# A convolution's stationary tile with its row pitch changed from 512 to 536 values, beside attention

## The chip, the cores and the metric

The kernel runs on one core of a Trainium2 chip. The metric is the device time of one execution in microseconds (us). Work is spread over five engines that run side by side: TensorE (PE, matmuls, with its weight loads listed as PEld), VectorE (DVE), ScalarE (ACT), GpSimd (POOL) and SyncE (SP, which here only issues DMAs). SBUF is the on-chip memory of 128 partitions from which the engines read, PSUM the one into which PE writes.

## The reference

Two independent blocks, whose outputs stand side by side in 1024 columns. All inputs are bf16, the sequence has S = 2048 rows and D = 512 columns.

Block A is attention with 32 heads of 16 values:

```
qkv = x @ wqkv                       # 2048x512 @ 512x1536
p = softmax(q k^T * 16**-0.5)        # per head, 2048x2048
a = concat_heads(p @ v) @ wo         # 2048x512
```

Block B is a short convolution with 4 taps, a gate, a long causal convolution and another gate, per column d:

```
k_shift[t] = sum of 4 taps of k around t, with weights shift_k[d]
kv = k_shift * v
y[t] = sum over s <= t of kv[s] * ssm_k[d, t - s]  +  kv[t] * ssm_D[d]
b = q * y
```

The reference computes the long convolution with Fourier transforms; the kernel computes it with matmuls.

## The kernel before

**Attention.** The scores are made in blocks of 128 keys x 512 queries for one head: 2048 blocks, taken in 692 chunks of three (in the first 56 chunks, of three and two by turns). For each chunk T, `emit_qk` (line 494) issues the QK matmuls into three PSUM banks; one ACT instruction (line 501) takes the exponential of the chunk into PT; two steps later `emit_pv` (line 566) multiplies by V. Chunks alternate between two sets of three banks, so the QK matmuls of chunk T wait until ACT is done with chunk T - 2. In many groups of 64 blocks, four blocks are taken from ACT and their exponential is computed on DVE by a polynomial (lines 519 to 535, with the tiles EI, EM, EH and PTD); in those chunks ACT has 1024 values per partition in place of 1536.

**Long convolution.** For each of the 512 columns d the kernel multiplies a Toeplitz matrix by the column of kv. The product kv lies in KV, `[128, NB, C]`: 128 positions on the partitions, NB = 16 blocks of 128 positions, C = 512 columns. For each d, `load_wr` (line 658) reads 128 shifted copies of the reversed kernel row from scratch memory in DRAM into one of the R_W = 12 rows of the ring WR, 512 KB each. Then come 16 lags n = 0 to 15: the stationary operand is `KV[:, n:NB, d]`, so 16 - n columns, one value from each block; the moving operand is 128 columns of WR. Four neighbouring columns d make a group and lie in four column groups of PE; the 128 groups run in order. `conv_lags` (line 669) issues lags n0 to n1 of a group:

```
ins = e.matmul(PS[32 * c:32 * c + NB - n, BGB, col:col + 128],
               lhsT=KV[:, n:NB, d],
               rhs=WR[:, d % R_W, 128 * (NB - 1 - n):128 * (NB - n)], ...
```

So a load for lag n reads 16 - n values of 2 bytes per partition, each C values further on than the last. When a group is done, its four rows of WR are loaded anew. After eight groups `conv_turn` (line 699) transposes the result, and DVE multiplies it by q and writes it back over the used columns of KV (line 712). `store_y` (line 715) sends it out, in 8 DMAs for each half of the columns.

**Before that,** KV holds the input x: four DMAs (`load_x`, line 191) bring it in, PE transposes it (`turn_x`, line 268, loads at line 276), and later DVE writes kv over it (`kv_chunk`, line 370, the write at line 385).

**Order of the work.** It is written out ahead by a planner in the kernel's own code. A loop over chunks T emits QK, PV and then `emit_bg(T)` (line 794): a unit of the attention's own projections, or up to LAGS = 5 lags of the convolution. The planner has times of its own for the loads of WR and for the chunks; when less than five lags come out, small matmuls on a zero tile ZR (`keep_busy`, line 773, matmul at line 780; their load has 16 columns that lie side by side) fill up. Each engine runs its list in order, with semaphores between them. All tiles are allocated at the start, one behind the other: KV comes after xT, KTo, QT, VAF, PT and WR and ahead of all others.

Of the kernel before, what the change touches and what calls it, by code (L numbers as in the profile page):

```python
# [23 lines left out]
C = 512  # L24
NB = S // 128
PAD = 128
LKZ = PAD + S
R_W = 12
R_PT = 4
R_O = 16  # L30
# [63 lines left out]
def bass_concat_heads__mha_block__ssm_conv_h3__prompt_kernel(  # L94
# [12 lines left out]
    x2, q2, k2, v2, out2 = A_x[0], B_q[0], B_k[0], B_v[0], out[0]  # L107
    kz_ap = nc.dram_tensor("kz_scratch", (C, LKZ), BF16).ap()

    ctxs = []  # L110

    def enter(cm):
        ctxs.append(cm)
        return cm.__enter__()

    def sem(name):
        return enter(nc.semaphore(name))

    def sb(name, shape, dt=BF16):
        return enter(nc.sbuf_tensor(name, shape, dt))  # L120
# [5 lines left out]
    VAF = sb("VAF", [128, KT, VROW])  # L126
    PT = sb("PT", [128, R_PT, 3 * QB])
    WR = sb("WR", [128, R_W, S])
    KV = sb("KV", [128, NB, C])
    QN = sb("QN", [128, NB, CH])  # L130
    WQP = sb("WQP", [128, 4, NG, 128])
    WKV = sb("WKV", [128, 2, 4, D])
# [18 lines left out]
    wr_flat = WR[:, :, :].rearrange("p r w -> p (r w)")  # L151
    KZS = wr_flat[:, 0:4 * LKZ].rearrange("p (c m) -> p c m", c=4)
    DSS = wr_flat[:, 4 * LKZ:4 * LKZ + 4].rearrange("p (c m) -> p c m", m=1)
    o1 = 5 * S
# [10 lines left out]
    pe, act, dve, pool, sp = [Eng(sem(n)) for n in ("s_pe", "s_act", "s_dve", "s_pool", "s_sp")]  # L165

    def dma(eng, dsem, outp, inp, deps=(), transpose=False):
        h = dsem.add()

        def fn(e):  # L170
            f = e.dma_start_transpose if transpose else e.dma_start
            f(outp, inp).then_inc(dsem.sem, 16)  # L172
        eng.op(fn, deps, inc=False)
        return h

    d_w = [DmaSem(sem(f"d_w{i}")) for i in range(5)]
    d_x = [DmaSem(sem(f"d_x{i}")) for i in range(4)]
# [6 lines left out]
    d_outA = [DmaSem(sem(f"d_outA{i}")) for i in range(R_A)]  # L184
    d_wr = [DmaSem(sem(f"d_wr{i}")) for i in range(R_W)]


    wview = A_wqkv.rearrange("(c p) f -> p c f", p=128)
    h_xn = [None] * 4

    def load_x(sc):
        h_xn[sc] = dma(sp, d_x[sc], KV[:, 4 * sc:4 * sc + 4, :],
                       x2[sc * 512:(sc + 1) * 512, :].rearrange("(t p) d -> p t d", p=128))
    load_x(0)
    h_wq = [dma(act, d_w[0], WST[:, :, 0:128], wview[:, :, 0:128])]
    h_wk = [dma(act, d_w[1], WK[:, :, 0:128], wview[:, :, D:D + 128])]
    load_x(1)
    h_wv = dma(act, d_w[2], WV, wview[:, :, 2 * D:3 * D])
    h_shk = dma(act, d_tap, SHK[:, :, :], B_shift_k.rearrange("(c p) m -> p c m", p=128))
# [12 lines left out]
    def load_kv(j, h_edge=None):  # L212
        b = kvbuf[(7 - j) % 3]
        deps = [h_kvfree.get(j + 3), h_edge]
        if j == 0:
            z = wr_flat[0:3, o1 + 5120 + 1024:o1 + 5120 + 4096]
            deps = [pool.op(lambda e: e.memset(z, 0.0), deps)]
        r0 = 2 * j * 128
        dma(sp, d_kv[j], b[4], v2[r0:r0 + 256, :].rearrange("(t p) d -> p t d", p=128), deps)
        for m in range(4):  # L220
            q = sp if m == 3 else pool
            ds = d_kv[j] if m == 3 else d_kp[j]
            if j == 0 and m > 0:
                h = dma(q, ds, b[m][m:128, 0, :], k2[0:128 - m, :], deps)
                src = bass.AP(tensor=k2.tensor, offset=k2[128 - m, 0].offset, ap=[[D, 128], [1, D]])
                h = dma(q, ds, b[m][:, 1, :], src, deps)
            else:
                src = bass.AP(tensor=k2.tensor, offset=k2[r0 - m, 0].offset, ap=[[D, 128], [128 * D, 2], [1, D]])
                h = dma(q, ds, b[m], src, deps)
            if m >= 2:  # L230
                h_kv[(j, m - 2)] = h
# [36 lines left out]
    def turn_x(sc, cp, bank, eng):  # L268
        pbf = PS[:, bank, :].bitcast(BF16)

        def fn(e):
            ins = None
            for i in range(2):
                for t in range(4):
                    c = 2 * cp + i
                    ins = e.transpose(pbf[:, 512 * i + 128 * t:512 * i + 128 * t + 128],
                                      KV[:, 4 * sc + t, 128 * c:128 * c + 128], IDN[:, :])
            return ins
# [11 lines left out]
    def pe_unit(u, bank, dcs=(0, 1, 2, 3)):  # L290
        kind = u[0]
        deps = [bank_free[bank]]
        if kind == "q":
            _, qb, g = u
            deps += h_x[qb] + [h_wqp[g]]

            def mm(e, dc):
                return e.matmul(PS[:, bank, :], lhsT=WQP[:, dc, g, :], rhs=xT[:, dc, qb * 512:(qb + 1) * 512],  # L298
                                start=(dc == 0), stop=(dc == 3))
        elif kind == "k":  # L300
            _, o, sc = u
            deps += h_x[sc] + [h_wk[min(o, 1)]]

            def mm(e, dc):
                return e.matmul(PS[:, bank, :], lhsT=WK[:, dc, o * 128:(o + 1) * 128],  # L305
                                rhs=xT[:, dc, sc * 512:(sc + 1) * 512], start=(dc == 0), stop=(dc == 3))
        else:
            _, kt = u
            deps += h_x[kt // 4] + [h_wv]

            def mm(e, dc):
                return e.matmul(PS[:, bank, :], lhsT=xT[:, dc, kt * 128:(kt + 1) * 128], rhs=WV[:, dc, :],  # L312
                                start=(dc == 0), stop=(dc == 3))

        def fn(e):
            ins = None
            for dc in dcs:
                ins = mm(e, dc)
            return ins
        return pe.op(fn, deps)  # L320
# [49 lines left out]
    def kv_chunk(j):  # L370
        b = kvbuf[(7 - j) % 3]
        st = {}

        def tap(m):
            in1 = TB[:, m:m + 1, :].broadcast_to([128, 2, D])
            st[m] = dve.op(lambda e: e.tensor_tensor(b[m], b[m], in1, ALU.mult),  # L376
                           [h_kv[(j, 0)], h_kv[(j, 1)], h_tb[m]])

        def add(m):
            st["a"] = dve.op(lambda e: e.tensor_tensor(b[3], b[3], b[m], ALU.add), [st[m], st[3], st.get("a")])  # L380

        def last():
            h = None
            for i in range(2):
                h = dve.op(lambda e, i=i: e.tensor_tensor(KV[:, NB - 1 - 2 * j - i, :], b[3][:, i, :], b[4][:, i, :],
                                                          ALU.mult), [st["a"], h_xt[0]])
            h_kvfree[j] = h
            h_kvc[0] = h
            if j >= 3:
                load_kv(j - 3)  # L390
        return [lambda m=m: tap(m) for m in (3, 2)] + [lambda: add(2), lambda: tap(1), lambda: add(1),
                                                       lambda: tap(0), lambda: add(0), last]
# [31 lines left out]
    h = pe_unit(("k", 0, 0), 7)  # L424
# [200 lines left out]
    def op_mm(qb, t, g0, g1, bank):  # L625
        dd = [h_wop[0], bank_free[bank] if g0 == 0 else None]
        dd += [h_otn[(qb * NG + g, 2 * (t // 2) + 2)] if g == NG - 1 and qb == NQB - 1 else h_otn[qb * NG + g]
               for g in range(g0, g1)]

        def fn(e):  # L630
            ins = None
            for g in range(g0, g1):
                ins = e.matmul(PS[:, bank, :], lhsT=OTN[:, oslot(qb * NG + g), t * 128:(t + 1) * 128], rhs=WOP[:, g, :],  # L633
                               start=(g == 0), stop=(g == NG - 1))
            return ins
        return pe.op(fn, dd)
# [21 lines left out]
    def load_wr(d):  # L658
        r = d % R_W
        deps = [h_kzw[0], h_kvc[0]] if d < R_W else [h_wrfree[d - R_W]]  # L660
        src = bass.AP(tensor=kz_ap.tensor, offset=kz_ap[d, 0].offset, ap=[[1, 128], [1, S]])
        h_wr[d] = dma(sp, d_wr[r], WR[:, r, :], src, deps)
# [6 lines left out]
    def conv_lags(qd, n0, n1):  # L669
# [5 lines left out]
        def fn(e):  # L675
            ins = None
            for n in range(n0, n1):
                for c in range(4):
                    d = 4 * qd + c
                    ins = e.matmul(PS[32 * c:32 * c + NB - n, BGB, col:col + 128],  # L680
                                   lhsT=KV[:, n:NB, d],
                                   rhs=WR[:, d % R_W, 128 * (NB - 1 - n):128 * (NB - n)],
                                   start=(n == 0), stop=(n == NB - 1), tile_position=(0, 32 * c))
            return ins
        h = pe.op(fn, deps)
        if n1 == NB:
            for c in range(4):
                h_wrfree[4 * qd + c] = h
                if 4 * qd + c + R_W < C:
                    load_wr(4 * qd + c + R_W)  # L690
# [8 lines left out]
    def conv_turn(b):  # L699
# [9 lines left out]
        yv = bass.AP(tensor=pbf.tensor, offset=pbf[:, NB - 1:NB].offset, ap=[pbf.ap[0], [-1, NB], [32, 32]])  # L709
        dst = KV[:, :, 32 * b:32 * b + 32]  # L710
        qv = QN[:, :, 32 * b % CH:32 * b % CH + 32]
# [3 lines left out]
    def store_y(i, t, hh):  # L715
        dst = out2[:, D + CH * i:D + CH * (i + 1)].rearrange("(t p) c -> p t c", p=128)
        dma(sp, d_outB[i], dst[:, t:t + 2, :], KV[:, t:t + 2, CH * i:CH * i + CH], [hh])

# [175 lines left out]
    for t in range(4):  # L894
        h = op_mm(qb, t, 7, 8, banks[t])
# [55 lines left out]
```

## Time and profile before

| What | Value |
|---|---|
| Runs | 925.15, 921.75, 929.33 us; median 925.15 |
| The profiled execution's own time | 924.61 us |
| Its span from the first to the last instruction | 922.8 us |
| Mean granted clock of TensorE | 0.993 |
| First exponential starts | 11.6 us |
| Convolution's matmuls | 126.9 to 880.5 us |
| Last exponential starts | 911.4 us |
| Data moved by DMA | 295.69 MB, 320 GB/s on the mean |

A row of a group gives source line, engine, operation, tile written and tile read, partitions x values, count; then busy time in us, mean duration of one in ns, idle time of the engine before them and who ended it. A form such as 128*16 on a load or matmul is 128 rows by 16 columns of the stationary operand. Loads and matmuls overlap, and so do successive activations: their durations don't add up to time. How fast ACT goes is read from the distance between starts. A row of the timeline has start in us, duration in us, then the same names and a count of merged instructions.

A row of the waits says who waited for whom, us in total, how often, the longest. A row of the windows has the stretch, its length, the busy time of PE, PEld, DVE, ACT and POOL with counts, granted clock, DMA share and GB/s.

### The profile page before, as it was taken

The page shows a single profiled execution, that of the slowest core. Times are in us where ns is not written, and L with a number is a line of the kernel's source. Part 1 is how long each engine was busy: PE and PEld are TensorE (multiplying, and loading weights), DVE is VectorE, ACT ScalarE, POOL GpSimd, SP SyncE. Part 2 cuts the span into 40 slices and gives each one's busy share as a digit, 9 for nine tenths or more (in the row PEclk, how much of TensorE's full clock was granted, in tenths as well). Part 3 has the DMA queues.
Part 4 walks back from the last instruction along what each step waited for, and adds up shares of the span by engine and source line. Part 5 has one row for each costly group of instructions (what it writes and reads, how often), then busy time and mean ns, then how long its engine had stood idle before and what let it go on. Part 6 is the DMA issues. An engine that isn't in the chain of part 4 may idle for free.

```text
span 922.8 us, 29902 instructions
## 1 busy us (share of the span) xinstructions
PE 758.8 (82%) x13615; PEld 349.7 (38%) x13664; DVE 638.9 (69%) x835; ACT 890.8 (97%) x698; POOL 38.2 (4%) x59
## 2 busy tenths in 40 slices
PE   8988888888888888888888788788878888778787
PEld 3332233334343434344434334344443334444422
DVE  4789617677677776777767577777677676677674
ACT  5999999999999999999999899999999999999996
POOL 3113030000000000000000000000000000000000
PEclk9999999999999999999999989999999999999999
DMA  9633569999999999999998999999999899999810
GB/s 312 239 139 114 195 196 325 353 358 372 372 341 372 326 379 352 384 357 352 355 395 307 344 394 390 361 389 339 395 366 364 313 338 381 404 377 365 331 47 23
DMA packets 96000, 295.69 MB, mean 320 GB/s; under 512 B 11525, under 2 KB 27906, under 8 KB 95490
## 3 DMA queue, kind: packets, MB, share of 16 engines
q1 hardware_dynamic: 90690, 284.33, 84.1%
q0 software_dynamic: 2784, 8.39, 2.6%
q8 instruction: 108, 1.77, 0.7%
q10 hardware_dynamic: 2400, 1.05, 0.4%
q14 instruction: 18, 0.15, 0.0%
HBM read 287.31 MB, written 6.42 MB: 318 GB/s over the span
## 4 chain that ended last, share of the span: by engine, by line
ACT 79%; PE 11%; DVE 5%; DMA 3%; issue 1%; SPq 0%; ACTq 0%
ACT PT L501 79%; DMA WR<-kz_scratch 3%; PE PS L494 3%; PE PS L566 2%; PE PS L633 2%; PE PS L312 2%; PE PS L305 1%; PE PS L680 1%; PE PS L298 1%; DVE WR L376 1%; DVE WR L380 1%; PE PS L417 1%; DVE KTo L335 1%; DVE VAF L341 0%; SPq L172 0%
## 5 line engine op out<-in xcount | busy, mean ns | idle before, releaser
L501 ACT ACTIVATE PT<-PS 128x1536 bf16<-128x1536 f32 (+1 forms) x692 | 886.8, 1577 | 15.7 <-PE PS L494 15.1
L494 PE MATMUL PS<-QT,KTo 32*128 32x512 bf16 x2048 | 272.1, 387 | 122.6 <-ACT PT L501 112.3
L680 PE MATMUL PS<-WR,KV 128*2 128x128 bf16 (+15 forms) x8192 | 301.6, 224 | 20.4 <-DMA WR<-kz_scratch 6.2
L566 PE MATMUL PS<-PT,VAF 128*32 128x512 bf16 x1936 | 289.4, 391 | 0.7 <-DVE VAF L341 0.5
L680 PEld LDWEIGHTS PS<-WR,KV 128*16 128x16 bf16 (+15 forms) x8192 | 195.9, 106 | 60.4 <-issue 40.3
L494 PEld LDWEIGHTS PS<-QT,KTo 32*128 32x128 bf16 x2048 | 67.4, 91 | 275.8 <-ACT PT L501 239.1
L530 DVE SCALAR_TENSOR_TENSOR EH<-EH,EM 128x1024 f32<-128x1024 f32 x112 | 141.7, 1265 | 3.1
L519 DVE TENSOR_SCALAR EI<-PS 128x512 int32<-128x512 f32 x112 | 78.9, 704 | 78.8 <-PE PS L494 77.4
L566 PEld LDWEIGHTS PS<-PT,VAF 128*32 128x32 bf16 x1936 | 68.8, 93 | 147.0 <-issue 138.2
L587 DVE STREAM_TRANSPOSE DT<-PS 128x512 f32<-128x512 f32 x31 | 22.7, 732 | 80.3 <-PE PS L566 80.3
L535 DVE SCALAR_TENSOR_TENSOR PTD<-EH,EI 128x1024 bf16<-128x1024 f32 x56 | 70.9, 1266 | 1.6
L530 DVE SCALAR_TENSOR_TENSOR EH<-EM 128x1024 f32<-128x1024 f32 x56 | 71.7, 1281 | 0.0
L780 PE MATMUL PS<-IDN,ZR 128*16 128x128 bf16 x724 | 52.4, 219 | 0.4 <-issue 0.3
L696 DVE CAST YB<-PS 128x256 bf16<-128x256 f32 x64 | 26.8, 419 | 27.5 <-PE PS L680 19.7
L523 DVE TENSOR_SCALAR EM<-EI 128x1024 int32<-128x1024 int32 x56 | 40.8, 729 | 1.5
L525 DVE TENSOR_SCALAR EI<-EI 128x1024 int32<-128x1024 int32 x56 | 39.4, 703 | 1.9
L326 DVE TENSOR_SCALAR QT<-PS 128x512 bf16<-128x512 f32 x32 | 22.0, 688 | 26.8 <-PE PS L298 26.7
L298 PE MATMUL PS<-xT,WQP 128*128 128x512 bf16 x102 | 32.1, 388 | 7.2 <-issue 3.7
L633 PE MATMUL PS<-WKV,OTN 128*128 128x512 bf16 x115 | 31.3, 381 | 2.4 <-issue 1.3
L172 POOL DMA_DIRECT2D out_dram<-OUTA x12 | 6.7, 555 | 622.0 <-DVE OUTA L640 609.5
L780 PEld LDWEIGHTS PS<-IDN,ZR 128*16 128x16 bf16 x724 | 28.0, 89 | 0.8 <-issue 0.8
L602 DVE STREAM_TRANSPOSE OTN<-OB 128x512 bf16<-128x512 bf16 (+1 forms) x33 | 23.6, 716 | 0.4
(66 smaller groups left out, 292.9 us busy)
## 6 DMA issues: line engine op xcount, KB each, us to landing
WR<-kz_scratch SPq DMA_DIRECT2D x512, 512.0 KB, 7.7
WR<-in_B_k_dram POOLq DMA_DIRECT2D x16, 256.0 KB, 4.4
kz_scratch<-WR SPq DMA_DIRECT2D x1, 2176.0 KB, 9.2
KV<-in_A_x_dram SPq DMA_DIRECT2D x4, 512.0 KB, 7.1
QN<-in_B_q_dram SPq DMA_DIRECT2D x8, 256.0 KB, 9.6
out_dram<-KV SPq DMA_DIRECT2D x16, 128.0 KB, 2.9
WR<-in_B_v_dram SPq DMA_DIRECT2D x6, 256.0 KB, 2.9
QT<-in_B_k_dram POOLq DMA_DIRECT2D x6, 256.0 KB, 4.7
```

The lines of the kernel that those rows point to most:

```text
L298: return e.matmul(PS[:, bank, :], lhsT=WQP[:, dc, g, :], rhs=xT[:, dc, qb * 512:(qb + 1) * 512], start=(dc == 0), stop=(dc == 3))
L494: ins = e.matmul(PS[:, bank, :], lhsT=KTo[32 * s:32 * s + 32, g // 2, kt * 128:(kt + 1) * 128], rhs=QT[32 * s:32 * s + 32, qb % 2, g, :], ...
L501: h_exp[T] = act.op(lambda e: e.activation(PT[:, T % R_PT, 0:n * QB], PS[:, banks[0]:banks[0] + n, :].rearrange("p b f -> p (b f)"), ACT.E ...
L519: h_fix[i] = dve.op(lambda e: e.tensor_scalar(EI[:, i % 2, :], PS[:, bank, :], FIX_LO, FIX_ADD, ALU.max, ALU.add), [h, h_pair.get(p - 1)])
L523: st["m"] = dve.op(lambda e: e.tensor_scalar(EM[:, :, :], EI[:, :, :], 0x7fffff, 0x3f800000, ALU.bitwise_and, ALU.bitwise_or), [h_fix[i], ...
L525: st["e"] = dve.op(lambda e: e.tensor_scalar(EI[:, :, :], EI[:, :, :], 0x7f800000, 0x40000000, ALU.bitwise_and, ALU.bitwise_xor), [st["m"]])
L530: st["h"] = dve.op(lambda e: e.scalar_tensor_tensor(EH[:, :, :], src, (B3, B2, B1)[j], m, ALU.add, ALU.mult), [st["m"], st.get("h")])
L535: lambda e: e.scalar_tensor_tensor(PTD[:, :, :], EH[:, :, :], B0, EI[:, :, :].bitcast(FP32), ALU.add, ALU.mult), [st["h"], st["e"], h_ptd. ...
L566: ins = e.matmul(PS[32 * s:32 * s + 32, pvb(qb * NG + g), :], lhsT=VAF[:, kt, h * VW:h * VW + 32], rhs=rhs, start=(kt == 0), stop=(kt == K ...
L633: ins = e.matmul(PS[:, bank, :], lhsT=OTN[:, oslot(qb * NG + g), t * 128:(t + 1) * 128], rhs=WOP[:, g, :], start=(g == 0), stop=(g == NG - 1))
L680: ins = e.matmul(PS[32 * c:32 * c + NB - n, BGB, col:col + 128], lhsT=KV[:, n:NB, d], rhs=WR[:, d % R_W, 128 * (NB - 1 - n):128 * (NB - n) ...
L780: ins = e.matmul(PS[32 * c:32 * c + 16, BGB, col:col + 128], lhsT=ZR[:, 0:16], rhs=IDN[:, :], start=False, stop=False, tile_position=(0, 3 ...
```

## The change

KV's rows get 24 values of padding that nothing reads or writes:

```diff
 LKZ = PAD + S
+CW = C + 24
...
-    KV = sb("KV", [128, NB, C])
+    KV = sb("KV", [128, NB, CW])
...
-        h_xn[sc] = dma(sp, d_x[sc], KV[:, 4 * sc:4 * sc + 4, :],
+        h_xn[sc] = dma(sp, d_x[sc], KV[:, 4 * sc:4 * sc + 4, 0:C],
...
-                h = dve.op(lambda e, i=i: e.tensor_tensor(KV[:, NB - 1 - 2 * j - i, :], b[3][:, i, :], b[4][:, i, :],
+                h = dve.op(lambda e, i=i: e.tensor_tensor(KV[:, NB - 1 - 2 * j - i, 0:C], b[3][:, i, :], b[4][:, i, :],
```

Two neighbouring columns of a stationary load thereby lie 536 x 2 = 1072 bytes apart in a partition, which is 67 lines of 16 bytes, where it was 1024 bytes or 64 lines. Every other access to KV keeps its shape with the new pitch. KV takes 16 x 48 = 768 bytes more per partition, and the tiles allocated after it move by as much. The order of instructions on every engine is the same, and so is the number of each.

## The prediction

> **What bounds the kernel now.** I read the page's totals and groups first, then the waits, then the groups by form inside the convolution's stretch, then single starts in the timeline.
>
> ```profile
> span 922.8 us, 29902 instructions
> PE 758.8 (82%) x13615; PEld 349.7 (38%) x13664; DVE 638.9 (69%) x835; ACT 890.8 (97%) x698; POOL 38.2 (4%) x59
> L501 ACT ACTIVATE PT<-PS 128x1536 bf16<-128x1536 f32 (+1 forms) x692 | 886.8, 1577 | 15.7 <-PE PS L494 15.1
> ```
> ```profile
> PE PS L494 <- ACT PT L501: 112.3, 316, 0.6
> ACT PT L501 <- PE PS L494: 15.1, 28, 3.3
> PE PS L680 <- DMA WR<-kz_scratch: 6.2, 5, 4.0
> ```
>
> ACT is busy for 97% of the span, nearly all of it in the exponentials of L501. PE waits 112.3 us for ACT, ACT only 15.1 us for PE. So an edit to PE's loads pays only where it changes how fast ACT goes. How fast ACT can go is read from starts of successive activations in the timeline (start, duration, engine, line):
>
> ```profile
> 199.09 1.02 ACT L501 ACTIVATE PT<-PS 128x1024 bf16<-128x1024 f32 x1
> 199.99 1.46 ACT L501 ACTIVATE PT<-PS 128x1536 bf16<-128x1536 f32 x1
> ...
> 883.81 1.44 ACT L501 ACTIVATE PT<-PS 128x1536 bf16<-128x1536 f32 x1
> 885.14 1.46 ACT L501 ACTIVATE PT<-PS 128x1536 bf16<-128x1536 f32 x1
> ```
>
> A short activation (1024 values) gives way after 0.90 us, a long one (1536) after 1.33 us, here after the convolution has ended; unrounded 0.905 and 1.331. Now the groups of ACT between 127 and 885 us, which is the convolution and its surroundings:
>
> ```profile
> L501 ACT ACTIVATE PT<-PS 128x1536 bf16<-128x1536 f32 x474 | 682.3, 1691 | 3.4 <-PE PS L494 2.9
> L501 ACT ACTIVATE PT<-PS 128x1024 bf16<-128x1024 f32 x108 | 138.0, 1278 | 4.3 <-PE PS L494 4.3
> ```
>
> At the clean pace these need 474 x 1.331 + 108 x 0.905 = 728.6 us; the stretch is 758 us long. ACT loses 29.4 us there, and only 7.7 us of it shows as idle time: the rest is activations that run long. This is the only pool from which the change can draw.
>
> **Where the loss sits.** One convolution step is a burst of 20 loads from KV with their matmuls, five lags of four. The loads have 16 columns at the first lag, one fewer at each next. Three successive long activations, and what ran beside the first and the second:
>
> ```profile
> 630.42 1.82 ACT L501 ACTIVATE PT<-PS 128x1536 bf16<-128x1536 f32 x1
> ...
> 632.02 1.57 ACT L501 ACTIVATE PT<-PS 128x1536 bf16<-128x1536 f32 x1
> ...
> 633.35 1.62 ACT L501 ACTIVATE PT<-PS 128x1536 bf16<-128x1536 f32 x1
> ```
> ```profile
> 630.42 1.49 DVE L530 SCALAR_TENSOR_TENSOR EH<-EM 128x1024 f32<-128x1024 f32 x1
> 630.62 0.38 PEld L680 LDWEIGHTS PS<-WR,KV 128*16 128x16 bf16 x20 [0.50 <-issue]
> 630.65 0.52 PE L680 MATMUL PS<-WR,KV 128*16 128x128 bf16 x20 [0.23 <-DVE QT L326]
> ...
> 632.64 0.47 PEld L680 LDWEIGHTS PS<-WR,KV 128*6 128x6 bf16 x20
> ```
> ```profile
> 350.36 1.22 DVE L530 SCALAR_TENSOR_TENSOR EH<-EM 128x1024 f32<-128x1024 f32 x1
> ```
>
> The second activation starts 1.60 us after the first, though its own scores lay ready; the third 1.33 us after the second. Beside the first ran a burst from 16 columns down, beside the second one from 6 columns down. The DVE instruction beside the wide burst took 1.49 us, the same one beside a narrow burst 1.22. L530 reads and writes SBUF alone, in tiles that PE doesn't touch. So ACT and DVE are each held up about 0.26 us while 16-column loads run; I take this as a collision in SBUF. The loads themselves, by form:
>
> ```profile
> L680 PEld LDWEIGHTS PS<-WR,KV 128*16 128x16 bf16 x512 | 26.9, 126 | 36.7 <-issue 35.1
> L680 PEld LDWEIGHTS PS<-WR,KV 128*15 128x15 bf16 x512 | 28.8, 148 | 0.1
> L680 PEld LDWEIGHTS PS<-WR,KV 128*11 128x11 bf16 x512 | 24.6, 117 | 1.8 <-issue 0.8
> L680 PEld LDWEIGHTS PS<-WR,KV 128*1 128x1 bf16 x512 | 18.2, 83 | 4.7 <-issue 0.3
> L780 PEld LDWEIGHTS PS<-IDN,ZR 128*16 128x16 bf16 x724 | 28.0, 89 | 0.8 <-issue 0.8
> ```
>
> A 16-column load with its columns side by side (ZR) takes 89 ns; from KV, with columns 1024 bytes apart, 126, at 15 columns even 148.
>
> **The change, part by part.**
>
> *Pitch of the loads (L680, 8192 of them).* Instructions, order and counts on every engine stay as they are; only addresses move. If the lines at a pitch of 64 fall on one part of the memory and those at 67 spread, the collision goes. I price it from the starts of L501. Of the long activations that did not wait for their scores, 142 had a burst of 14 or more columns beside them; the first and last of these, each with the start that follows:
>
> ```profile
> 130.73 1.72 ACT L501 ACTIVATE PT<-PS 128x1536 bf16<-128x1536 f32 x1
> 132.09 1.72 ACT L501 ACTIVATE PT<-PS 128x1536 bf16<-128x1536 f32 x1
> ...
> 876.62 1.80 ACT L501 ACTIVATE PT<-PS 128x1536 bf16<-128x1536 f32 x1
> 877.94 1.83 ACT L501 ACTIVATE PT<-PS 128x1536 bf16<-128x1536 f32 x1
> ```
>
> Summed over the 142, their intervals exceed 1.331 by 13.6 us. One, at 525 us, holds 3.7 us of a wait for data and is left out: 9.9 us, 0.07 us each (from nothing up to 0.26). With 11 to 13 columns 71 activations lose 0.7 us in all, with 10 or fewer 241 lose 1.2. The loss follows the columns. Bounds: 0 (no collision goes) and 9.9 + 0.7 + 1.2 + 1.5 (non-waiting short ones) = 13.3. I take 9.9 + 0.7 = 10.6, since the narrow bursts show that the loss vanishes when the loads are light.
>
> *PE's own bursts.* The wide burst above spans 0.52 us for 20 matmuls, 0.30 without the last one's 0.22. The narrower one below spans 0.40 for 16, so 0.18 for three steps and 0.24 for four:
>
> ```profile
> 640.93 0.40 PE L680 MATMUL PS<-WR,KV 128*11 128x128 bf16 x16
> ```
>
> 0.06 to 0.07 us per wide burst is hidden by PE's 112.3 us of waiting, except where a short activation has run out before PE is done: 13 such places, 0.9 us. Bounds 0 and 0.9; I take 0.9.
>
> *Loads into the ring.* ACT's pace paces the convolution, and this the loads of WR. What is late next is those loads:
>
> ```profile
> 200.00:800.00 600.00, 493.67 (x9928) 239.34 (x9962) 429.95 (x528) 594.10 (x462) 6.66 (x12) 0.99 0.98 363
> 780.00:820.00 40.00, 31.78 (x752) 17.01 (x749) 28.59 (x37) 39.90 (x33) 0.00 (x0) 1.00 1.02 396
> ```
>
> The last two columns are DMA share and GB/s: 363 on the mean, 396 in one stretch, so 1.5% more is to be had. The ring holds three of 128 groups; 10.6 / 128 x 3 = 0.25 us less per turn. If the five waits of 6.2 us each grow by that, 1.2 us come back; bounds 0 and 3 (a dozen late groups in place of five); I take 1.0.
>
> *Rows that start off a power of two.* The x loads and y stores touch KV in rows of 1072 bytes, and whatever is allocated behind KV moves by 16 x 48 = 768 bytes.
>
> ```profile
> KV<-in_A_x_dram SPq DMA_DIRECT2D x4, 512.0 KB, 7.1
> out_dram<-KV SPq DMA_DIRECT2D x16, 128.0 KB, 2.9
> 520.68 8.21 DMA WR<-kz_scratch
> ```
>
> Only the first x load and the eight y stores near 516 to 532 us lie on the path; the latter push the WR load that the chain of waits shows at 520.68. 128 KB at 363 GB/s are 0.36 us; were a store half as long again, eight cost 1.4 us, and a tenth on the x load 0.7. Bounds 0 and 2; I take 0, as the pieces stay 1024 and 512 bytes long. DVE's writes to KV (L385, L712) have nothing waiting on them that ACT needs, and cost 0.
>
> **Sum.** The profiled run took 924.61 us (span 922.8, 1.8 around it), 0.5 below the median of 925.15. 924.6 - 10.6 - 0.9 + 1.0 = 914.1.
>
> [...] The rows above have ACT's interval at 1.60 us beside a wide burst and 1.33 beside a narrow one. [...]
>
> **The rivals.**
>
> 1. The change doesn't do what it says. Between 1 and 16 columns a KV load grows by 43 ns, 2.9 per column. If that is the price of a separate line per column, 67 lines cost what 64 do: each column still has a line of its own, the wide bursts stay as dense, ACT is held up as before, and the time is 924.6. For it: ZR's 16 columns in two or three lines take 89 ns. Against it: 15 columns take longer than 16, and two other engines are held. [...]
>
> 2. Slower: the spread reaches everyone. Now, loads of 13 columns and fewer cost ACT almost nothing. If a spread load meets every stream that ACT, DVE and the moving rows run through, instead of one part of the memory, the narrow bursts do what the wide ones do: 71 + 161 further activations (those with 11 to 13 and with 1 to 10 columns) at 0.07 us give 16 us, 941. It decides once narrow bursts cost ACT over 0.04 us each. Against it: loads that finish sooner occupy less.
>
> 3. DMA takes the gain. If the loads cannot go faster than now, ACT waits for PE, and PE for WR: 922 to 924. Against it: the 396 GB/s.
>
> **How the numbers follow.** The forecast, collision gone: 0.62, between 908 (13.3 + 0.9, with a few tenths of the waits also gone, and the spread of the runs) and 919 (half of the wide loss gone); most of that, 0.45, is over 1% under 925. Rivals 1 and 3: 0.23, 922 to 927. Rival 2: 0.15, of which hardly any within 1%. 1% is about what a measurement of this kernel tells from no change. Faster 0.45; same 0.17 + 0.23 = 0.40; slower 0.15. The range 907 to 929 leaves out rival 2 and little else.
>
> **What would show it.** Right: KV loads of 16 columns near 90 to 105 ns and no hump at 15; L530's longest near 1.25 us; ACT's two groups between 127 us and the end of the convolution within 18 to 20 us of the clean pace; wide bursts of 20 matmuls in 0.46 us. Wrong: 126 and 148 ns unchanged with L530 still up to 1.49 (rival 1); loads of few columns longer than now and L530 long beside them (rival 2); more than 6.2 us of waits for WR with clean activations (rival 3).

## The result and the profile after

The changed kernel takes 914.78 us (median of 6 runs, 909.98 to 916.77) against 922.32 us for the kernel before (6 runs, of which the three shown ahead are the first); the ratio is 0.9897, with a 95% interval of 0.9857 to 0.9937. The forecast was 914.1, within 907 to 929. The profiled execution took 915.37 us, 9.2 less than the one before. All line numbers behind 27 are one higher than before; in the experiments the matmul that reads KV stands in lines 680 to 684.

The page's totals and the group of the exponentials after:

```profile
span 913.6 us, 29902 instructions
PE 758.2 (83%) x13615; PEld 345.1 (38%) x13664; DVE 621.8 (68%) x835; ACT 879.1 (96%) x698; POOL 37.9 (4%) x59
L502 ACT ACTIVATE PT<-PS 128x1536 bf16<-128x1536 f32 (+1 forms) x692 | 875.2, 1509 | 17.8 <-PE PS L495 16.9
```

PE's busy time did not move (758.8 to 758.2). ACT's fell by 11.7 us and DVE's by 17.1, though the change touches no instruction of ACT, and of DVE only the places that two of its instructions write. That is the first sign of where the time came from. The groups of ACT in the convolution's stretch, 127 to 876 us:

```profile
L502 ACT ACTIVATE PT<-PS 128x1536 bf16<-128x1536 f32 x475 | 667.7, 1609 | 5.6 <-PE PS L495 4.8
L502 ACT ACTIVATE PT<-PS 128x1024 bf16<-128x1024 f32 x108 | 129.7, 1201 | 4.4 <-PE PS L495 4.4
```

At the clean pace of the forecast these need 475 x 1.331 + 108 x 0.905 = 730.0 us, and the stretch is 749 us long: 19.0 us are lost where it was 29.4. The idle part grew from 7.7 to 10.0 us, so more than the whole gain is activations that no longer run long.

The same chunk that the forecast took as its example, in the timeline of the changed kernel: three successive starts of ACT, then what ran beside the first of them.

```profile
619.36 1.69 ACT L502 ACTIVATE PT<-PS 128x1536 bf16<-128x1536 f32 x1
620.69 1.70 ACT L502 ACTIVATE PT<-PS 128x1536 bf16<-128x1536 f32 x1
622.02 1.71 ACT L502 ACTIVATE PT<-PS 128x1536 bf16<-128x1536 f32 x1
```
```profile
619.39 1.22 DVE L531 SCALAR_TENSOR_TENSOR EH<-EM 128x1024 f32<-128x1024 f32 x1
619.59 0.34 PEld L681 LDWEIGHTS PS<-WR,KV 128*16 128x16 bf16 x20 [0.49 <-issue]
619.62 0.48 PE L681 MATMUL PS<-WR,KV 128*16 128x128 bf16 x20 [0.23 <-DVE QT L327]
```

The wide burst is there as before, but the activation beside it gives way after 1.33 us instead of 1.60, the DVE instruction takes 1.22 instead of 1.49 us, and the burst itself 0.48 instead of 0.52. Over all instances (shortest, median, longest in ns), first before and then after:

```profile
L530 DVE SCALAR_TENSOR_TENSOR EH<-EH,EM x112: 1215/1226/1458, 146.6 to 906.8; 128x1024 f32<-128x1024 f32 x112
L530 DVE SCALAR_TENSOR_TENSOR EH<-EM x56: 1199/1220/1485, 145.4 to 904.3; 128x1024 f32<-128x1024 f32 x56
...
L519 DVE TENSOR_SCALAR EI<-PS x112: 652/692/896, 138.4 to 902.2; 128x512 int32<-128x512 f32 x112
```
```profile
L531 DVE SCALAR_TENSOR_TENSOR EH<-EH,EM x112: 1211/1225/1227, 144.8 to 897.6; 128x1024 f32<-128x1024 f32 x112
L531 DVE SCALAR_TENSOR_TENSOR EH<-EM x56: 1210/1218/1220, 143.5 to 895.0; 128x1024 f32<-128x1024 f32 x56
...
L520 DVE TENSOR_SCALAR EI<-PS x112: 651/691/693, 138.2 to 893.0; 128x512 int32<-128x512 f32 x112
```

Medians stand still, and the long tail is gone. The means of the three groups fell by 2 to 5% only; the longest against the median (1485 against 1220 ns in the second) shows a delay that comes and goes. The loads after, by form (busy us, then the mean in ns):

```profile
L681 PEld LDWEIGHTS PS<-WR,KV 128*16 128x16 bf16 x512 | 23.5, 110 | 37.6 <-issue 35.5
L681 PEld LDWEIGHTS PS<-WR,KV 128*15 128x15 bf16 x512 | 23.0, 116 | 0.5 <-issue 0.3
L681 PEld LDWEIGHTS PS<-WR,KV 128*11 128x11 bf16 x512 | 21.5, 102 | 3.1 <-issue 1.5
L681 PEld LDWEIGHTS PS<-WR,KV 128*1 128x1 bf16 x512 | 18.4, 83 | 4.8 <-issue 0.3
```

16 columns went from 126 to 110 ns, 15 from 148 to 116, one column stayed at 83.

### The profile page after: what moved, and what is told of

Read it like the earlier page. It is cut to its first block, busy times and chain, and to the rows that moved or that the text cites. A ratio compares the mean times of both kernels' runs of the same rounds, so it can differ in the third digit from the quotient of the medians.

```text
span 913.6 us, 29902 instructions
## 1 busy us (share of the span) xinstructions
PE 758.2 (83%) x13615; PEld 345.1 (38%) x13664; DVE 621.8 (68%) x835; ACT 879.1 (96%) x698; POOL 37.9 (4%) x59
## 4 chain that ended last, share of the span: by engine, by line
ACT 75%; PE 14%; DVE 6%; DMA 3%; issue 2%; SPq 0%; ACTq 0%
ACT PT L502 75%; PE PS L495 4%; DMA WR<-kz_scratch 3%; PE PS L567 2%; PE PS L681 2%; PE PS L634 2%; PE PS L313 2%; DVE EH L531 1%; PE PS L306 1%; DVE WR L377 1%; DVE WR L381 1%; PE PS L418 1%; PE PS L299 1%; DVE KTo L336 1%; SPq L173 0%
## 5 line engine op out<-in xcount | busy, mean ns | idle before, releaser
L502 ACT ACTIVATE PT<-PS 128x1536 bf16<-128x1536 f32 (+1 forms) x692 | 875.2, 1509 | 17.8 <-PE PS L495 16.9
L681 PE MATMUL PS<-WR,KV 128*8 128x128 bf16 (+15 forms) x8192 | 302.8, 222 | 24.5 <-DMA WR<-kz_scratch 7.1
L681 PEld LDWEIGHTS PS<-WR,KV 128*16 128x16 bf16 (+15 forms) x8192 | 190.1, 96 | 69.1 <-issue 46.4
L531 DVE SCALAR_TENSOR_TENSOR EH<-EH,EM 128x1024 f32<-128x1024 f32 x112 | 137.0, 1223 | 3.1
L520 DVE TENSOR_SCALAR EI<-PS 128x512 int32<-128x512 f32 x112 | 76.9, 687 | 79.3 <-PE PS L495 77.3
L536 DVE SCALAR_TENSOR_TENSOR PTD<-EH,EI 128x1024 bf16<-128x1024 f32 x56 | 68.5, 1224 | 1.6
L531 DVE SCALAR_TENSOR_TENSOR EH<-EM 128x1024 f32<-128x1024 f32 x56 | 68.2, 1217 | 0.0
L781 PE MATMUL PS<-IDN,ZR 128*16 128x128 bf16 x724 | 54.3, 223 | 1.2 <-issue 1.0
L524 DVE TENSOR_SCALAR EM<-EI 128x1024 int32<-128x1024 int32 x56 | 38.7, 692 | 1.5
```

Source lines behind the costliest of these rows:

```text
L502: h_exp[T] = act.op(lambda e: e.activation(PT[:, T % R_PT, 0:n * QB], PS[:, banks[0]:banks[0] + n, :].rearrange("p b f -> p (b f)"), ACT.E ...
L520: h_fix[i] = dve.op(lambda e: e.tensor_scalar(EI[:, i % 2, :], PS[:, bank, :], FIX_LO, FIX_ADD, ALU.max, ALU.add), [h, h_pair.get(p - 1)])
L524: st["m"] = dve.op(lambda e: e.tensor_scalar(EM[:, :, :], EI[:, :, :], 0x7fffff, 0x3f800000, ALU.bitwise_and, ALU.bitwise_or), [h_fix[i], ...
L531: st["h"] = dve.op(lambda e: e.scalar_tensor_tensor(EH[:, :, :], src, (B3, B2, B1)[j], m, ALU.add, ALU.mult), [st["m"], st.get("h")])
L536: lambda e: e.scalar_tensor_tensor(PTD[:, :, :], EH[:, :, :], B0, EI[:, :, :].bitcast(FP32), ALU.add, ALU.mult), [st["h"], st["e"], h_ptd. ...
L781: ins = e.matmul(PS[32 * c:32 * c + 16, BGB, col:col + 128], lhsT=ZR[:, 0:16], rhs=IDN[:, :], start=False, stop=False, tile_position=(0, 3 ...
```

## The experiments

The theory is a guess of the author's: if the memory had parts that repeat with the address, a load whose columns all meet one part could hold up ACT and DVE there. No view shows such parts; the runs show what a pitch does to the times. Pitches are counted in units of 16 bytes, called lines; whether the memory is made of such lines, no run shows. The first rival: the place of the tiles behind KV, which moved by 768 bytes, made ACT and DVE faster. The second: columns that lie apart cost ACT time whatever the pitch, and something else changed. The third: the loads of WR set the pace.

All runs but the last two are collected in one table. "ACT's loss" is the forecast's measure: the long activations that did not wait for their scores and had a burst of 14 columns or more beside them, their intervals over 1.331 us summed, without single waits over 0.6 us. Before, that is 141 intervals; after, 135, of which these are the first and the last, each with the start that follows:

```profile
130.66 1.69 ACT L502 ACTIVATE PT<-PS 128x1536 bf16<-128x1536 f32 x1
131.99 1.71 ACT L502 ACTIVATE PT<-PS 128x1536 bf16<-128x1536 f32 x1
...
867.41 1.77 ACT L502 ACTIVATE PT<-PS 128x1536 bf16<-128x1536 f32 x1
868.76 1.76 ACT L502 ACTIVATE PT<-PS 128x1536 bf16<-128x1536 f32 x1
```

| Kernel | Pitch in lines | Modulo 16 | Load of 16, of 15 columns, ns | Longest EH instruction, us | ACT's loss, us | Ratio to before, 95% interval |
|---|---|---|---|---|---|---|
| before | 64 | 0 | 126, 148 | 1.49 | 9.9 | 1 |
| changed | 67 | 3 | 110, 116 | 1.23 | 0.6 | 0.9897, 0.9857 to 0.9937 |
| e1_tail_gap | 64 | 0 | 126, 148 | 1.49 | 10.5 | 0.9989, 0.9963 to 1.0015 |
| e2_pitch65 | 65 | 1 | 107, 113 | 1.23 | 0.3 | 0.9895, 0.9849 to 0.9941 |
| e3_pitch68 | 68 | 4 | 107, 114 | 1.23 | 0.0 | 0.9877, 0.9818 to 0.9935 |
| e4_pitch72 | 72 | 8 | 116, 128 | 1.23 | 0.1 | 0.9897, 0.9853 to 0.9941 |
| e7_pitch16 | 16 | 0 | 126, 150 | 1.47 | 10.2 | 1.0062, 1.0039 to 1.0086 |
| e8_side_by_side | none | | 87, 88 | 1.23 | 0.1 | 0.9880, 0.9848 to 0.9912 |
| e5_fewer_loads_512 | 64 | 0 | 126, 146 | 1.48 | 10.3 | 0.9930, 0.9903 to 0.9956 |
| e6_fewer_loads_536 | 67 | 3 | 110, 116 | 1.23 | 0.2 | 0.9808, 0.9775 to 0.9841 |

The measure still holds intervals at whose end ACT waited up to 0.6 us for scores. Counted without these (the last score matmul over 0.1 us before the next start), the loss beside wide bursts is 10.1 us before, 10.3 to 10.6 in the other runs at 64 and 16 lines, and 0.0 to 0.2 in all the rest; the largest single one is 0.26 us before and 0.02 after. A pitch is said to collide where the times are those of before: loads of 16 columns at 126 ns, the longest EH at 1.47 us or more, ACT's loss near 10 us.

### Is it the pitch, or the place of the later tiles?

The pitch stays at 512 values, and the 768 bytes stand behind KV as a tile that nothing uses.

```diff
     KV = sb("KV", [128, NB, C])
+    GAP = sb("GAP", [128, NB, 24])
```

> KV keeps its pitch of 64 lines; the 768 bytes stand as an unused tile behind KV, so every later tile moves as in the change. Theory (the pitch of the loads did it): as before, 921 to 926 us, 16-column KV loads near 126 ns, the polynomial's instructions (EH) up to 1.48 us. Rival (the move of EI, EM, EH and the other tiles did it): 912 to 916 us, EH no longer than 1.23 us, loads near 126 ns all the same.

It took 923.85 us, not to be told from before. Its loads and longest DVE instructions are those of before:

```profile
L681 PEld LDWEIGHTS PS<-WR,KV 128*15 128x15 bf16 x512 | 28.7, 148 | 0.1
L681 PEld LDWEIGHTS PS<-WR,KV 128*16 128x16 bf16 x512 | 27.0, 126 | 36.6 <-issue 34.3
```
```profile
L531 DVE SCALAR_TENSOR_TENSOR EH<-EM x56: 1204/1219/1490, 144.0 to 904.6; 128x1024 f32<-128x1024 f32 x56
```

So the place of the later tiles is not the cause. What is left is the pitch, which the next runs vary.

### Which pitches collide?

The padding is changed alone: 8, 32 and 64 values in place of 24. For the last, the output ring OUTA was cut from four rows to two, so that the tiles fit.

```diff
-CW = C + 24
+CW = C + 8      # e2: 65 lines
+CW = C + 32     # e3: 68 lines
+CW = C + 64     # e4: 72 lines, with R_A = 2
```

> Pitch of 65 lines, odd like 67. Theory (lines at a multiple of some power of two share a part of the memory, odd pitches spread over all parts): as with 67, 912 to 917 us, 16-column loads near 110 ns, EH no longer than 1.23 us. Rival (the later tiles' place counts, here moved by 256 bytes): between before and after. Rival (67 is special): loads well over 110 ns.

> Pitch of 68 lines, a multiple of four. Theory with 16 parts or more: the 16 columns still meet four parts or more, loads between 110 and 120 ns, EH up to 1.25 to 1.35 us, 914 to 920 us. With 8 parts: two parts, loads near 118 to 126, EH to 1.4. With 4 parts: as before, loads at 126 ns, EH up to 1.48 us, 921 to 926 us. Rival (any pitch that is not exactly 1024 bytes will do): as with 67.

> Pitch of 72 lines, a multiple of eight; so that it fits, the ring of output tiles OUTA has two rows in place of four (12 outputs in 690 chunks, expected to cost under 1 us). Theory with 8 parts: as before, loads at 126 ns, EH up to 1.48 us, 921 to 926 us. With 16 parts: two of them, loads near 118, EH up to 1.4 us. With 32 or more: near 68's. Rival (any pitch that is not exactly 1024 bytes will do): as with 67, 912 to 917 us.

They took 914.95, 913.39 and 914.47 us, the kernel before beside them 923.34. With 65 lines it came out as expected. With 68 and 72 the collision with ACT and DVE was expected to come back in part, and did not: EH stays at 1.23 us in both, ACT's loss at 0.0 and 0.1 us, and the loads at 68 lines take 107 ns, as the rival has it by which any pitch but exactly 1024 bytes will do. But the loads of the last are slower again than with 67, 116 against 110 ns at 16 columns and 128 against 116 at 15:

```profile
L681 PEld LDWEIGHTS PS<-WR,KV 128*15 128x15 bf16 x512 | 24.9, 128 | 0.3 <-issue 0.3
L681 PEld LDWEIGHTS PS<-WR,KV 128*16 128x16 bf16 x512 | 24.6, 116 | 38.2 <-issue 36.5
```

So 72 is not like 64 (the pitch modulo 8 lines does not settle it), nor as free as 68. The next experiment comes from the other side: KV is laid out as four slabs of 128 columns, so that a load's columns are 256 bytes apart.

```diff
+G = 4
+W = C // G
-    KV = sb("KV", [128, NB, C])
+    KV = sb("KV", [128, G, NB, W])
...
-                                   lhsT=KV[:, n:NB, d],
+                                   lhsT=KV[:, d // W, n:NB, d % W],
```

> KV laid out as four slabs of 128 columns, so that the columns of a load lie 256 bytes, 16 lines, apart; no padding. The x loads become 16 DMAs of 128 KB with pieces of 256 bytes, the y stores 32, which may cost 1 to 4 us at the start and near 520 us. What the loads show: if the parts repeat after 16 lines, all columns meet one part, as at 64: loads near 126 ns, EH up to 1.48 us, 921 to 928 us. If after 32 lines, two parts; after 64 lines, four parts: loads at 115 to 122 ns, EH at most 1.3 us, 912 to 920 us. Rival (what hurts is a pitch of exactly 1024 bytes): loads near 107 ns.

It took 929.48 us, beside 925.2 for the kernel before; a little more than expected. The start accounts for 4.5 us: the x loads are 16 DMAs with pieces of 256 bytes, and the first exponential starts at 16.1 us in place of 11.6. The loads take 126 and 150 ns:

```profile
L683 PEld LDWEIGHTS PS<-WR,KV 128*15 128x15 bf16 x512 | 28.2, 150 | 0.0
L683 PEld LDWEIGHTS PS<-WR,KV 128*16 128x16 bf16 x512 | 26.6, 126 | 41.1 <-issue 39.2
```
```profile
L533 DVE SCALAR_TENSOR_TENSOR EH<-EH,EM x112: 1214/1226/1474, 149.5 to 910.3; 128x1024 f32<-128x1024 f32 x112
```

A pitch of 16 lines collides as 64 does, so it is not the 1024 bytes as such. Loads of 16 and 15 columns take 126 and 150 ns at 16 lines, 116 and 128 at 72 (8 modulo 16), 107 and 114 at 68 (4 modulo 16); ACT's loss is 10.2, 0.1 and 0.0 us. Of the six pitches of the table, the two that are multiples of 16 lines, 256 bytes, collide with ACT and DVE, and at 72 the loads alone are slower than at the other three. The theory with a period of 16 lines fits this, but neither the parts nor their period are shown by any run: that remains the author's guess, and a longer period is not ruled out.

### Does a line for each column go on costing something?

The kernel before, with each load's columns taken side by side from one block; the y half is then computed from other values.

```diff
-                                   lhsT=KV[:, n:NB, d],
+                                   lhsT=KV[:, n, min(d, C - NB + n):min(d, C - NB + n) + NB - n],
```

> The kernel before, but each load takes its 16 - n columns side by side from one block of KV (other values than the convolution needs, so the y half is not the reference's). Theory (the loss was columns that meet in one part of the memory; a line of its own for each column costs PE only time that is hidden): loads of 16 columns near 90 ns, EH at most 1.23 us, 911 to 916 us, as with a pitch of 67. Rival (a line for each column goes on costing ACT with 67 lines too): 903 to 910 us.

It took 912.8 us, within the spread of the kernels with 65 to 72 lines. Its loads:

```profile
L680 PEld LDWEIGHTS PS<-WR,KV 128*16 128x16 bf16 x512 | 19.5, 87 | 40.3 <-issue 37.5
...
L680 PEld LDWEIGHTS PS<-WR,KV 128*15 128x15 bf16 x512 | 17.8, 88 | 0.4 <-issue 0.2
```

So the 126 ns of a load before come in two steps: from 87 ns with the columns side by side to 107 to 110 with the columns 1040, 1072 or 1088 bytes apart, which stays, and from 110 to 126 (116 to 148 at 15 columns) for the collision, which the change removed. Only the second reached ACT: its loss is 0.1 us with the columns side by side, 0.0 to 0.6 with 65, 67 and 68 lines and 9.9 with 64. The first is 20 to 23 ns for 16 columns. That it is a price for each column in a line of its own was the author's reading; no columns between 2 and 256 bytes apart were run, so this is not shown.

### What do the loads of WR take back?

Both kernels with every fourth group's loads of WR left out, so that a quarter of the convolution's columns use rows of an earlier group.

```diff
     def load_wr(d):
         r = d % R_W
+        if d >= R_W and d // 4 % 4 == 3:
+            h_wr[d] = h_wr[d - R_W]
+            return
```

> The kernel before, with the loads of WR left out for every fourth group after the first turn of the ring (those matmuls use the rows that lie there, so a quarter of the convolution's columns are not the reference's). A quarter less DMA. Theory (ACT bounds, DMA only adds waits at a few groups): 916 to 921 us, waits of PE for WR under 2 us, 16-column loads still near 126 ns and EH up to 1.48 us. Rival (the loads of WR set the pace): under 900 us.

> The changed kernel with the same quarter of the loads of WR left out. To be held against the run before it. Theory (DMA took back about 1 us of the gain): 10 to 12 us less than the kernel with 512 values and fewer loads. Rival (DMA took back several us of it): 13 us or more less. Rival (DMA took nothing, the gain of ACT is only 8 to 9): 8 to 9 us less.

918.33 and 906.27 us: 12.1 us between them, just over the 10 to 12 expected. A quarter fewer loads of WR is worth only 7 us to the kernel before, so the loads do not set the pace. PE's waits, by kernel (before; changed; fewer loads with 512; fewer loads with 536):

```profile
PE PS L680 <- DMA WR<-kz_scratch: 6.2, 5, 4.0
PE PS L680 <- issue: 3.1, 5, 1.0
```
```profile
PE PS L681 <- DMA WR<-kz_scratch: 7.1, 8, 3.2
PE PS L681 <- issue: 6.8, 9, 1.3
```
```profile
PE PS L683 <- DMA WR<-kz_scratch: 0.4, 1, 0.4
PE PS L683 <- issue: 0.3, 1, 0.3
```
```profile
PE PS L684 <- DMA WR<-kz_scratch: 1.9, 3, 1.0
PE PS L684 <- issue: 1.4, 5, 0.4
```

With all loads, the change adds 0.9 us of waits for WR and 3.7 us of stops for which the profile names no cause; with a quarter fewer, 1.9 and 1.4 us remain of the two, so the second kind goes with the DMA load as well. In the changed kernel its nine stops stand before matmuls in the middle of a burst, which wait for no semaphore; what causes them was not found. How much of this reaches the end can't be settled from the times: 12.1 us with fewer loads, and with all loads 7.5 us in the first comparison and 14.3 in the last (below), the kernel before having moved between 922.3 and 927.3 from one comparison to the next.

### A version that goes further?

What DMA still holds is largest near 516 us, where eight stores of y go out beside the loads; PE waits 3.23 us for WR before its matmuls at 519.63. The changed kernel with these stores 12 chunks apart, and the changed kernel as it is, were run side by side.

```diff
-                    later.append((T + 1 + t, lambda i=i, t=t: store_y(i, t, hh)))
+                    later.append((T + 1 + (1 if i else 6) * t, lambda i=i, t=t: store_y(i, t, hh)))
```

> The changed kernel, with the eight stores of the first half of y sent every 12 chunks in place of every 2, so that they don't crowd the loads of WR near 516 us. If that crowding is the largest piece that DMA still holds (in the changed kernel 3.1 us of lost ACT time near 516 and 1.1 at 521, after a chain of 7.9 us of WR load): 909 to 912 us, 3 to 5 us under the changed kernel run beside it. If the loads of WR are late there for another reason (the 2 MB of q that are loaded at the same time, or the ring as such): within 1.5 us of it.

> The changed kernel once more, beside the run with spread stores: 912 to 917 us, 0.988 to 0.993 of the kernel before.

Medians 910.89 (907.04 to 913.83) and 912.99 (910.42 to 914.57) us; ratios to before of 0.9828 (0.9799 to 0.9856) and 0.9852 (0.9825 to 0.9880). The ranges of the two overlap, so the 2.1 us are not shown, and they lie between what the two theories expected. Between 505 and 535 us ACT lost 2.5 us in place of 3.9; but the first profile of the changed kernel had 5.1 there, so this too is within what two runs of one kernel differ by. And the chain of waits has a WR load there all the same (start, us, what):

```profile
508.19 7.97 DMA WR<-kz_scratch
```

So the stores are at most part of what is late there. The q loads at the same place were not tried.

## Why the prediction was right

*Pitch of the loads, 10.6 us.* Right, and shown: of the 9.9 us beside wide bursts 0.6 remain with 67 lines (0.0 to 0.3 with 65, 68 and 72), and they come back in full at a pitch of 16 lines (10.2). The 0.7 us counted for bursts of 11 to 13 columns went in part. Without intervals whose end waited for scores they are 0.73 before, 0.25 after and 0.07 with columns side by side. Of the waits that have to be kept out there, the largest after the change is this, 0.72 us over the clean pace (two starts, with ACT's idle time before the second):

```profile
768.58 1.45 ACT L502 ACTIVATE PT<-PS 128x1536 bf16<-128x1536 f32 x1
770.63 1.45 ACT L502 ACTIVATE PT<-PS 128x1536 bf16<-128x1536 f32 x1 [0.60 <-PE PS L495]
```

*PE's own bursts, 0.9 us.* Not shown. The wide burst of the example shrank by 0.04 us (0.52 to 0.48), not 0.06 to 0.07: a load of 16 columns fell from 126 to 110 ns, and the step from 87 ns, with columns side by side, to 110 stayed. But ACT's waits for PE did not get shorter, 15.1 us before and 16.9 after:

```profile
ACT PT L502 <- PE PS L495: 16.9, 33, 2.6
```

Beside the convolution, the intervals that ended in a wait for scores lost 18.4 us before and 19.4 after. Those under 0.6 us fell from 11.0 to 10.5, so 0.5 us at most of PE's own gain shows there; the longer ones grew from 7.4 to 8.9.

*Loads into the ring, 1.0 us back.* Right in direction: waits for WR grew by 0.9 us. Stops without a named cause, 3.7 us more, were not foreseen.

*The sum.* In the two profiles, from the convolution's first load to its last, the intervals that waited for nothing lost 10.2 us less and the waiting ones 1.0 more: 9.2 together, which is what the profiled executions differ by. The forecast had 10.5. That 914.1 lies so near the median of 914.78 is partly luck: it was worked from 924.6, but the kernel before took 922.3 in the comparison. So the medians differ by 7.5 us there, and by 14.3 in the last comparison; the first one's interval alone goes from 6 to 13.

*Rows off a power of two, 0.* The x loads still land after 7.1 us, the stores after 3.0 (2.9 before), DVE's L713 writes KV in 692 ns as before. Nothing came of it. That nothing waits on these writes was not quite so: PE waited 1.6 us in all for L712 before, and 1.5 for L713 after.

*ACT beside PE's loads.* With only the pitch of KV changed, ACT's interval in the example went from 1.60 to 1.33 us: the loads did hold it up.

*The rivals.* The first had a true half, the 20 to 23 ns by which a load of columns apart stays above one of columns side by side, and failed on the other: the distance does count (126 ns at 64 lines, 110 at 67). The second, that spread loads disturb everyone, is refuted: no DVE instruction of EH exceeds 1.23 us at any spread pitch, and bursts of 10 columns or fewer cost ACT 0.3 us in all after the change. The third took a part: its sign, over 6.2 us of waits for WR with clean activations, was met with 7.1, but it did not take the gain.

*The signs named ahead* for the forecast came out but for three: the 16-column load was put at 90 to 105 ns and measures 110, the wide burst at 0.46 us and measures 0.48, and the hump at 15 columns shrank from 22 to 6 ns instead of going. ZR's 89 ns was the wrong yardstick for a load whose columns still lie apart; the run with columns side by side, at 87 ns, shows this.

## What to carry to other kernels

Look at the longest instance of an instruction beside its median (1485 against 1220 ns here), and at what ran on the other engines in that moment; here the tail on DVE went when the addresses of PE's loads changed. A stationary operand whose columns lay 1024 or 256 bytes apart cost ACT about 10 us here, and from 1024 bytes 8 values of padding per row took this down to 0.3. Judge an edit to an engine with slack by what it does to the engine that bounds, and not by its own busy time: PE's hardly moved (758.8 to 758.2 us).

## What was new about the hardware

PE's stationary loads held up ACT and DVE here, and it depended on the pitch of their columns: with 64 and 16 lines, 1024 and 256 bytes, ACT lost 9.9 and 10.2 us beside wide bursts and EH took up to 1.49 and 1.47 us; with 65, 67, 68 and 72 lines ACT lost at most 0.6 us and EH took at most 1.23. At 72 the loads of 16 columns took 116 ns, against 107 to 110 at the other three, and ACT lost no more for it (0.1 us). Why the two multiples of 256 bytes differ from the four other pitches, no run here shows. The loss rises steeply with the columns: before, where ACT didn't wait for its scores, bursts from 9 columns down cost it less than 0.01 us each on the mean, those from 10 columns 0.02, from 11 or 12 columns 0.01, and those from 16 columns 0.07 on the mean and up to 0.26. Why loads of 15 columns take longer than those of 16 (148 and 126 ns), and whether loads in one column group alone would collide, no run here shows either.
